# A fused forward and backward kernel: the loads of its start in another order, the transposes of grad_out between their products, and ten blocks of those products ahead of the spectral part

## The chip, the cores and the metric

The kernel runs on one core of a Trainium2 chip. The metric is device time in microseconds (us) of one execution. A core has five engines that work from queues of their own: PE (matmul), DVE (vector), ACT (scalar), POOL (general) and SP, which here only sends transfers. PE's results land in PSUM banks, and ACT or DVE must empty a bank before PE can fill it again. Each engine takes its instructions strictly in the order that the built program gives it.

## The reference: what is computed

The forward part, with S = 2048 tokens, D = 1024 features and F = 3584 hidden units:

```python
mod = (_silu(c) @ w_mod).reshape(c.shape[0], 6, 1, -1)
sa, ca, ga, sb, cb, gb = (mod[:, 0], mod[:, 1], mod[:, 2], mod[:, 3], mod[:, 4], mod[:, 5])
h = _layernorm(x, axis=-1) * (1 + ca) + sa
x = x + ga * _A_ref(h, A_w_r, A_w_i)      # rfft2, times (w_r + i w_i), irfft2
h = _layernorm(x, axis=-1) * (1 + cb) + sb
x = x + gb * _B_ref(h, B_w1, B_b1, B_w2, B_b2)   # layernorm, w1, gelu, w2
```

The outputs are x and the gradients of all inputs for a given `grad_out`. The first step of the backward part needs nothing of the forward part: the gradient that reaches the hidden units, d_ph = (gb * grad_out) w2ᵀ, can be computed as soon as the row gb of `mod` is there. All of this change lies around that product.

## The kernel before, in words

**Rows of mod.** Each of the six rows (0 sa, 1 ca, 2 ga, 3 sb, 4 cb, 5 gb) is computed in two halves. `mod_load` brings 1 MB of weights into one of three tiles in a ring (`wblk`), and `mod_block` (L247) does 8 matmuls (`pm`, L253) with it. Rows 1 and 5 are computed first, row 0 behind the transposes, rows 2, 3 and 4 later.

**gBoT.** `grad_out` comes in four quarters of 512 tokens, `gos[0..3]` (`load_go`). PE transposes each 128x128 piece into a PSUM bank (`pt`, L344, 32 transposes for each quarter, 4 to a bank), and on the way out DVE (L347) and ACT (L351) in turn multiply with the column gb (`gb_col`, made of the row by eight small matmuls `pc`, L337). The result is `gBoT[j]`, j = 0..3.

**pp.** `ph_part(fc, js)` (L673) computes block fc of 28 of d_ph: for each j, eight matmuls (`pp`, L679) of w2ᵀ with `gBoT[j]`, 896 in all, evacuated to `pho` and sent to DRAM (`d_ph`) by POOL. w2ᵀ comes by transposing loads on SP, two blocks to a load, two tiles in turn (`wt`, `load_w2t`, L301). `PH_EARLY` = 6 blocks stand in the program ahead of the spectral part. The other blocks are filler: the scheduler puts their matmuls where PE has nothing else in the spectral part. Of the last four blocks, the j = 2, 3 halves stand in the plan of the next stage.

**x.** Four chunks of 512 rows are loaded (`load_tok`), on SP and on POOL, and go through LayerNorm. `ln_dve` (L437 to L439) takes the statistics on DVE alone, eight for a chunk; `ln_mix` (L447 to L455) takes four on DVE and the others as sums on ACT. `ln_fin` (L427) does the square root on ACT, `norm_act` (L461) the four norms of a chunk on ACT. Then DVE multiplies with the row and folds tokens and features (`fold_tok`, `fold_d`) into `fbuf`. Chunk 0 uses `ln_dve`, the others `ln_mix`.

**Spectral part.** `spectral_core` does the transforms as matmuls: `pu` (L471, 128 matmuls on `fbuf`), `pcs`, a product with the filter on DVE (`R`), `pv`, `po`. Its results are taken by `consume_fwd` (L721), four times: residual, `ln_mix`, `norm_act` from `xt` to `ct`, two products with rows, `ln_dve` on `ct`, `norm_act` from `ct` to `ct`, and a store to `d_n3` on SP.

**The z stage.** `z_block(b, g, g + 1)` (L783) computes 32 matmuls (`pz`, L797) of w1 with the transposed n3 (`n3Ta`, `n3Tb`), four banks, evacuated by ACT (L800), and then the gelu and its derivative: three long ACT operations for a block (L802, L806, L808) between DVE products (L173) and sums (L817). z(b, g) below is such a block. `bo_pass` (L830) does the `pbo` matmuls with w2. The plan (L882) is written out by hand:

```python
plan = [("z", 0, 0)] + [("p", fc, 0) for fc in range(PH_KEEP, NFC)] + [("z", 0, 1), ("z", 0, 2), ("z", 0, 3)]
```

and goes on with `pbo` and further z blocks in turn. So the join of the parts is z(0,0), 64 `pp`, z(0,1), z(0,2), z(0,3), then `pbo` and z(0,4), `pbo` and z(0,5). The loads of w1 are ordered behind the last w2ᵀ load (L751). The rest of the kernel is the backward part.

**What sets the order.** The program is written in one order, and a scheduler gives each engine its own: within `tc.high_priority()` work goes ahead, `tc.issue_after(x)` puts an instruction behind x, and `nc.any` lets the scheduler choose ACT or DVE. So an edit of the start can change the order of ACT and DVE far behind it.

Of the kernel before, what the change touches and what calls it, by code (L numbers as in the profile page):

```python
# [17 lines left out]
P = 128  # L18
# [17 lines left out]
def kernel(  # L36
# [200 lines left out]
    wring = [0]  # L237

# [8 lines left out]
    def mod_block(r, h, wblk=None):  # L247
# [4 lines left out]
        for jc in range(NDC):  # L252
            nc.tensor.matmul(pm[:], lhsT=u_b[:, jc, :], rhs=wblk[:, jc, :], start=(jc == 0), stop=(jc == NDC - 1))  # L253
# [86 lines left out]
    for j in range(4):  # L340
        for cch in range(NDC):
            pt = psum.tile([P, BW], BF16, tag="f", name="pt", bufs=4)
            for a in range(4):
                nc.tensor.transpose(pt[:, a * P:(a + 1) * P], gos[j][:, a, cch * P:(cch + 1) * P], ident[:])  # L344
            if cch % 2 == 0:
                with tc.high_priority():
                    nc.vector.tensor_scalar(out=gBoT[j][:, cch, :], in0=pt[:], scalar1=gb_col[:, cch:cch + 1], scalar2=0.0,  # L347
                                            op0=ALU.mult, op1=ALU.add, accum_out=gu[:, j, cch:cch + 1])
            else:
                with tc.high_priority():  # L350
                    nc.scalar.activation(out=gBoT[j][:, cch, :], in_=pt[:], func=ACT.Identity, scale=gb_col[:, cch:cch + 1],  # L351
                                         accum_out=gu[:, j, cch:cch + 1])

# [297 lines left out]
    for h in range(2):  # L651
        mod_block(0, h)
# [9 lines left out]
    nc.vector.tensor_scalar(out=sar[:, 0], in0=sar[:, 0], scalar1=4.0, scalar2=None, op0=ALU.mult)  # L662
    fold_d(saf.rearrange("p (c d) -> p c d", c=1), sar[:, 0], sar[:, 1])


    pho = reg.tile([P, 3, 4, BW], BF16, name="pho", tag="ot")
    phs = [pho[:, k] for k in range(3)] + [reg.tile([P, 4, BW], BF16, name="phr", tag="ph")[:]]
    last_pe = [None]

    def ordered():  # L670
        return tc.issue_after(last_pe[0].ins)

    def ph_part(fc, js):  # L673
        fg, k = fc // 2, fc % 2
        ph2 = phs[fc % 4]
        for j in js:
            pp = ps_f("pp")
            for cch in range(NDC):
                last_pe[0] = nc.tensor.matmul(pp[:], lhsT=wt[:, fg % 2, cch, k * P:(k + 1) * P], rhs=gBoT[j][:, cch, :],  # L679
                                              start=(cch == 0), stop=(cch == NDC - 1))  # L680
            q = (0, 2, 3, 1)[j]
            ov = ph2[:, :, q * P:(q + 1) * P]
            pv = pp[:, :].rearrange("p (i w) -> p i w", w=P)
            if j % 2 == 0:
                with tc.high_priority():
                    nc.any.tensor_copy(out=ov, in_=pv)
            else:
                with tc.high_priority():
                    nc.any.tensor_copy(out=ov, in_=bass.AP(tensor=pv.tensor, offset=pv.offset + 511, ap=[pv.ap[0], [-P, 4], [-1, P]]))
        if js[-1] == 3:  # L690
            nc.gpsimd.dma_start(out=d_ph[fc * P:(fc + 1) * P, :], in_=ph2.rearrange("p i w -> p (i w)"))

    PH_EARLY = 6
    late_mods = [(r, h) for r in (2, 3, 4) for h in range(2)]
    for fc in range(PH_EARLY):
        ph_part(fc, (0, 1, 2, 3))
        if fc % 2 == 1:
            load_w2t(fc // 2 + 2)
            if fc > 1:
                with tc.issue_after(last_pe[0].ins):  # L700
# [640 lines left out]
```

## Time and profile before

| | |
|---|---|
| median of the runs | 1483.12 us (1481.81 to 1483.87) |
| profiled execution | 1487.43 us, span 1485.5 us |
| PE busy | 1402.2 us, 94% |
| DVE busy | 1069.0 us, 72% |
| ACT busy | 720.3 us, 48% |
| POOL busy | 362.6 us, 24% |
| granted clock of PE, mean | 0.98 |
| read from and written to DRAM | 162.06 MB and 111.20 MB |

Times in the text are counted from the start of the span. A row of a time line gives start, length, engine, line of the kernel, operation, result and operands, the count of instructions put together in the row, and in square brackets the idle time ahead of it and what ended it. A group's name gives tiles without their numbers: `pz` is the bank of a z block. Lines of the kernel before are used for its rows.

Landmarks of before, from the time line of PE: the transposes end at 45.49, the unbroken run of `pu` begins at 128.56, z(0,0) at 346.84, z(0,4) at 392.17, z(0,5) at 406.77.

### The profile page before, as it was taken

Reading aid. Unit: us, or ns where it says so; the run is one execution under the profiler, and the core shown is the slowest. Engines: PE = TensorE matmul, PEld = TensorE weight load, DVE = VectorE, ACT = ScalarE, POOL = GpSimd, SP = SyncE. Lnnn points to the kernel's source line nnn. Section 1 sums busy time; section 2 is a strip of 40 time slices with the busy share of each in tenths; the row PEclk is TensorE's granted clock in tenths of the full one; section 3 lists DMA queues with packets and bytes.
Section 4 is the critical chain, followed back from the end, with each engine's and each line's share of the span. In section 5 each row is a group of like instructions: output and inputs, shape, how many; then the busy total and the mean of one; then the engine's idle time right before and its main releaser. Section 6 shows DMA issues by size and latency. Waiting matters only on the chain.

```text
span 1485.5 us, 18204 instructions
## 1 busy us (share of the span) xinstructions
PE 1402.2 (94%) x6703; PEld 653.7 (44%) x6835; DVE 1069.0 (72%) x1574; ACT 720.3 (48%) x960; POOL 362.6 (24%) x421
## 2 busy tenths in 40 slices
PE   5889989999899999999999999997999999899998
PEld 2434545444344444444344444443444444444443
DVE  5883786898799788887420899986367677888533
ACT  4765546857886756666202333332522444453211
POOL 5620541211113122212111001112134421322323
PEclk8999999999999999999999999999999999999999
DMA  9982563899776876797898266477499977565994
GB/s 335 274 226 61 150 224 122 267 245 338 252 237 213 260 241 219 236 275 230 237 290 253 97 218 227 145 209 196 127 210 246 261 229 213 161 198 154 267 222 169
DMA packets 358046, 324.27 MB, mean 218 GB/s; under 512 B 209066, under 2 KB 300736, under 8 KB 357702
## 3 DMA queue, kind: packets, MB, share of 16 engines
q1 hardware_dynamic: 324166, 207.71, 51.9%
q0 software_dynamic: 33792, 115.40, 22.5%
q8 instruction: 53, 0.87, 0.2%
q14 instruction: 35, 0.29, 0.1%
HBM read 162.06 MB, written 111.20 MB: 184 GB/s over the span
## 4 chain that ended last, share of the span: by engine, by line
PE 32%; DVE 31%; issue 16%; DMA 9%; ACT 8%; POOL 4%; SPq 0%; POOLq 0%; DVEq 0%; ACTq 0%
PE pbo L846 9%; PE pz L797 5%; DVE ct L173 5%; DVE gt L173 4%; PE pu L471 4%; PE pg L943 3%; PE gw2acc L1064 3%; PE pv L564 3%; DVE got L1027 2%; DMA out_dram<-otl 2%; PE gw1acc L1240 1%; ACT ct L461 1%; PE pp L679 1%; DVE st L437 1%; DVE w2sA L817 1%
## 5 line engine op out<-in xcount | busy, mean ns | idle before, releaser
L679 PE MATMUL pp<-gBoT,wt 128*128 128x512 bf16 x878 | 197.4, 381 | 6.4 <-DMA wt<-in_B_w_dram 2.8
L1240 PE MATMUL gw1acc<-gzh,n3n 128*128 128x512 bf16 x876 | 195.2, 381 | 1.2 <-issue 0.2
L943 PE MATMUL pg<-w1T,gzr 128*128 128x512 bf16 x876 | 194.6, 379 | 1.6 <-ACT gn3b L951 0.2
L797 PEld LDWEIGHTS <-w 128*128 128x128 bf16 x896 | 87.6, 98 | 112.5 <-issue 9.0
L679 PEld LDWEIGHTS <-wt 128*128 128x128 bf16 x896 | 88.0, 99 | 110.8 <-issue 6.0
L1240 PEld LDWEIGHTS <-n3n 128*128 128x128 bf16 x896 | 87.7, 98 | 105.7 <-issue 2.5
L943 PEld LDWEIGHTS <-gzr 128*128 128x128 bf16 x896 | 86.8, 98 | 107.9 <-issue 4.9
L797 PE MATMUL pz<-n3Ta,w 128*128 128x512 bf16 x437 | 99.5, 383 | 6.1 <-ACT gt L800 4.1
L1064 PE MATMUL gw2acc<-gB,hhsA 128*128 128x512 bf16 x438 | 99.5, 384 | 3.4 <-DMA hhsA<-d_hh 2.1
L797 PE MATMUL pz<-n3Tb,w 128*128 128x512 bf16 x439 | 98.4, 379 | 0.5
L846 PEld LDWEIGHTS <-hhA 128*128 128x128 bf16 x608 | 59.6, 99 | 74.5 <-issue 5.8
L806 ACT ACTIVATE gt<-gt 128x2048 bf16<-128x2048 bf16 x28 | 53.5, 1910 | 70.9 <-DVE gt L173 70.9
L800 ACT ACTIVATE gt<-pz,b_col 128x512 bf16<-128x512 f32 x112 | 72.8, 684 | 29.1 <-PE pz L797 27.1
L1244 ACT CAST gwo<-gw1acc 128x512 bf16<-128x512 f32 x53 | 30.8, 584 | 115.4 <-PE gw1acc L1240 96.6
L173 DVE TENSOR_TENSOR gt<-gt,gt 128x2048 bf16<-128x2048 bf16 x56 | 68.5, 1223 | 21.6 <-ACT gt L808 20.9
L1069 ACT CAST gwo<-gw2acc 128x512 bf16<-128x512 f32 x54 | 29.9, 583 | 110.9 <-DMA out_dram<-gwo 75.6
L173 DVE TENSOR_TENSOR ct<-ct 128x2048 bf16<-128x2048 bf16 x64 | 75.8, 1219 | 10.7 <-ACT ct L632 8.8
L1064 PEld LDWEIGHTS <-hhsA 128*128 128x128 bf16 x448 | 44.0, 99 | 56.4 <-DMA hhsA<-d_hh 3.8
L987 DVE CUSTOM_DVE_ANT_0 otl<-otl 128x1024 bf16<-128x1024 bf16 x24 | 29.0, 1223 | 51.7 <-DMA otl<-in_w_mod_dram 45.3
L802 ACT ACTIVATE gt<-gt 128x2048 bf16<-128x2048 bf16 x28 | 53.4, 1907 | 0.6
L808 ACT ACTIVATE gt<-gt 128x2048 bf16<-128x2048 bf16 x28 | 53.4, 1907 | 0.5
L1245 POOL DMA_DIRECT2D out_dram<-gwo x56 | 30.7, 550 | 79.6 <-ACT gwo L1244 59.3
(313 smaller groups left out, 2508.5 us busy)
## 6 DMA issues: line engine op xcount, KB each, us to landing
gzr<-d_gz SPq DMA_DIRECT2D x28, 512.0 KB
wblk<-in_w_mod_dram SPq DMA_DIRECT2D x12, 1024.0 KB
out_dram<-otl POOLq DMA_DIRECT2D x48, 256.0 KB
d_ph<-pho POOLq DMA_DIRECT2D x21, 512.0 KB
d_hh<-hhA POOLq DMA_DIRECT2D x19, 512.0 KB
w2sD<-in_B_w_dram SPq DMA_DIRECT2D x14, 512.0 KB
hhC<-d_ph SPq DMA_DIRECT2D x14, 512.0 KB
w2sA<-d_ph SPq DMA_DIRECT2D x14, 512.0 KB
```

The costliest lines, as they stand in the source:

```text
L173: return nc.vector.tensor_tensor(out=out, in0=a, in1=b, op=op)
L471: last_pu[0] = nc.tensor.matmul(pu[:], lhsT=fb[:, i, cl, c8 * P:(c8 + 1) * P], rhs=sm[:, i, :], start=(i == 0), stop=(i == 3))
L679: last_pe[0] = nc.tensor.matmul(pp[:], lhsT=wt[:, fg % 2, cch, k * P:(k + 1) * P], rhs=gBoT[j][:, cch, :], start=(cch == 0), stop=(cch == ...
L797: last_pe[0] = nc.tensor.matmul(pz[:], lhsT=w1s[g][:, cch, k * P:(k + 1) * P], rhs=n3T[:, cch, :], start=(cch == 0), stop=(cch == NDC - 1))
L800: nc.scalar.activation(out=zb[:, k, :], in_=pz[:], func=ACT.Identity, bias=b1_col[:, fc:fc + 1], scale=1.0)
L802: nc.scalar.activation(out=av, in_=zb, func=ACT.Square)
L806: nc.scalar.activation(out=sg, in_=bv, func=ACT.Sigmoid, scale=2.0 * GK)
L808: nc.scalar.activation(out=bv, in_=bv, func=ACT.Sigmoid, scale=-2.0 * GK)
L846: last_pe[0] = nc.tensor.matmul(pbs[i][:], lhsT=hh[:, k, i * P:(i + 1) * P], rhs=wp[:, k, :], start=False, stop=(g == 6 and k == 3))
L943: last_pg[0] = nc.tensor.matmul(pgs[i][:], lhsT=gzs[b, g][:, k, i * P:(i + 1) * P], rhs=w1Ts[g][:, k, h * KH:(h + 1) * KH], start=(g == 0 ...
L1064: nc.tensor.matmul(acc[:], lhsT=hh_of(fc)[:, t, :], rhs=gBs[t // 4][:, t % 4, h * KH:(h + 1) * KH], start=(t == 0), stop=(t == NT - 1))
L1240: nc.tensor.matmul(acc[:], lhsT=n3ns[t // 4][:, t % 4, cch * P:(cch + 1) * P], rhs=gz2[t // 8][:, t % 8, :], start=(t == 0), stop=(t == NT ...
```

## The change

- **Loads on SP.** Before: c, w(1,0), x0, w(1,1), w(5,0), go0, w(5,1), wt0, go1, x1, go2, go3, x2, x3, wt1, then rows 0, 2, 3, 4. After: c, w(5,0), w(5,1), go0, wt0, go1, go2, go3, x0, wt1, w(1,0), w(1,1), x1, x2, w(0,0), x3, wt2, w(0,1), w(2,0) and so on. (w(r,h) is half h of row r of the weights, wt0 the first w2ᵀ load.)
- **PE at the start.** Row 5 first, then the transposes of go0 and go1, the `pp` of j = 0 for blocks 0 and 1 (16 matmuls), the transposes of go2, `pp` of j = 1, the transposes of go3, `pp` of j = 2 and of j = 3. These are tied to that order by `issue_after`.
- **Ten blocks.** `PH_EARLY` is 10. Blocks 2 to 9 follow, with rows (1), (0), (2, and half of 3), (the rest of 3, and 4) of mod between them. In the built order of PE, 264 `pp` stood ahead of the last 120 of the 128 `pu`; now 320 stand ahead of all 128.
- **LayerNorm of x.** The chunk i = 0 stands behind the last DVE evacuation of gBoT, the chunks 1 to 3 behind PE instructions of blocks 1 to 3; which functions they use is as before.
- **What follows from it in the built order.** PE does the same matmuls. ACT has one more table load (8 for 7). At the join, ACT's queue before had the square root and the four last norms of chunk 3 one by one between evacuations of z(0,2) and z(0,3). After, the order of ACT is: two norms of x (`ct<-xt`), the four evacuations of z(0,2), the other two norms of x, two gelu steps, table load and square root, all four last norms (`ct<-ct`), table load, two gelu steps, and then the evacuations of z(0,3).

Cut to its core:

```diff
-    mod_get(1, 0)
-    load_tok(x4s[0], A_x, 0)
-    mod_get(1, 1)
     mod_get(5, 0)
-    for h in range(2):
-        mod_block(1, h, wm[1, h][:])
     mod_get(5, 1)
     load_go(0)
     load_w2t(0)
-    load_go(1)
-    load_tok(x4s[1], A_x, 1)
-    load_go(2)
-    load_go(3)
+    for j in range(1, 4):
+        load_go(j)
     for h in range(2):
         mod_block(5, h, wm[5, h][:])
+    load_tok(x4s[0], A_x, 0)
+    load_w2t(1)
+    mod_get(1, 0)
+    mod_get(1, 1)
+    load_tok(x4s[1], A_x, 1)
     load_tok(x4s[2], A_x, 2)
+    mod_get(0, 0)
+    mod_get(0, 1)
     load_tok(x4s[3], A_x, 3)
-    load_w2t(1)
...
+    def ordered():
+        return tc.issue_after(last_pe[0].ins)
+
+    def ph_part(fc, js):
...
+                with ordered() if fc < 2 else ExitStack():
+                    last_pe[0] = nc.tensor.matmul(pp[:], lhsT=wt[:, fg % 2, cch, k * P:(k + 1) * P], rhs=gBoT[j][:, cch, :],
+                                                  start=(cch == 0), stop=(cch == NDC - 1))
...
+    def go_turned(j):
         for cch in range(NDC):
             pt = psum.tile([P, BW], BF16, tag="f", name="pt", bufs=4)
             for a in range(4):
-                nc.tensor.transpose(pt[:, a * P:(a + 1) * P], gos[j][:, a, cch * P:(cch + 1) * P], ident[:])
+                with ordered() if last_pe[0] is not None else ExitStack():
+                    last_pe[0] = nc.tensor.transpose(pt[:, a * P:(a + 1) * P], gos[j][:, a, cch * P:(cch + 1) * P], ident[:])
...
+    go_turned(0)
+    for j in range(4):
+        if j < 3:
+            go_turned(j + 1)
+        for fc in range(2):
+            ph_part(fc, (j,))
...
-    PH_EARLY = 6
-    late_mods = [(r, h) for r in (2, 3, 4) for h in range(2)]
+    PH_EARLY = 10
+    early_mods = [None, [(1, 0), (1, 1)], None, [(0, 0), (0, 1)], None, [(2, 0), (2, 1), (3, 0)], None, [(3, 1), (4, 0), (4, 1)], None, None]
+    ln_at = {0: gbo_in[0]}
     for fc in range(PH_EARLY):
-        ph_part(fc, (0, 1, 2, 3))
+        if fc > 1:
+            ph_part(fc, (0, 1, 2, 3))
         if fc % 2 == 1:
             load_w2t(fc // 2 + 2)
...
+        for r, h in early_mods[fc] or ():
+            with ordered():
+                mod_block(r, h, wm[r, h][:] if r < 2 else None)
+        if fc in (1, 2, 3):
+            ln_at[fc] = last_pe[0]
...
     for i in range(4):
         x4, fb = x4s[i], fbuf[:, i]
-        if i == 0:
-            with tc.issue_after(u_in.ins):
-                ln_dve(x4, 0, i)
-        elif i > 0:
-            ln_mix(x4, 0, i, fb)
-        else:
-            ln_act(x4, 0, i, fb)
+        with tc.issue_after(ln_at[i].ins):
+            (ln_mix(x4, 0, i, fb) if i > 0 else ln_dve(x4, 0, i))
         norm_act(fb, x4, 0, i)
```

More of the change, by code (lines that the diff above doesn't have):

```diff
@@ L237 @@
     wring = [0]
+    last_pe = [None]
     def mod_tile():
@@ L661 @@
     to_cols(b1_col[:], b1r, NFC, ident[:])
[L662 to L686, printed above, removed]
-            else:
[L688 to L691, printed above, removed]
```

37 lines of the change are left out of this document (26 added, 11 removed).

## The prediction

> **What bounds the kernel now.** I read the page's busy shares first, then the time line of PE, then those of ACT and DVE at the places where PE stands still. The shares:
>
> ```profile
> PE 1402.2 (94%) x6703; PEld 653.7 (44%) x6835; DVE 1069.0 (72%) x1574; ACT 720.3 (48%) x960; POOL 362.6 (24%) x421
> ```
>
> PE leaves only 83 us of 1485.5. Busy time by stretches up to the spectral part (start and end, length, then busy us of PE, PEld, DVE, ACT, POOL; then granted clock, DMA share, GB/s) shows where a third of that lies:
>
> ```profile
> 0.00:20.00 20.00, 7.39 (x22) 2.69 (x23) 10.11 (x28) 3.23 (x5) 16.60 (x35) 0.93 0.92 326
> 20.00:40.00 20.00, 12.35 (x108) 8.48 (x108) 12.33 (x34) 16.04 (x29) 7.12 (x10) 0.82 1.03 350
> ...
> 120.00:128.50 8.50, 7.85 (x36) 3.45 (x36) 7.70 (x8) 2.93 (x5) 0.87 (x2) 1.00 0.28 90
> ```
>
> All stretches to 128.5 sum to 100.4 us of PE: 28 us idle. In the first 40 us the DMA share is 0.92 to 1.03, so this start waits for loads. But the spectral part begins when LN and fold of x are done, on DVE. The time line of DVE there (start, length, operation, count):
>
> ```profile
> 65.21 5.36 DVE L452 TENSOR_SCALAR mv<-mv 128x2 f32<-128x2 f32 x2
> 68.81 1.76 DVE L173 TENSOR_TENSOR fbuf<-x 128x2048 bf16<-128x2048 bf16 x1
> ...
> 126.72 0.69 DVE L173 TENSOR_TENSOR fbuf<-fbuf,sb_saf 128x1024 bf16<-128x1024 bf16 x1
> ```
>
> And of POOL at the first of these rows:
>
> ```profile
> 61.57 8.98 POOL L412 TENSOR_SCALAR em<-em 128x2048 bf16<-128x2048 bf16 x1
> ```
>
> The last piece of fbuf ends at 127.41, and the unbroken run of pu starts at 128.56. The time line of PE, from there to the first blocks of z:
>
> ```profile
> 128.56 12.25 PE L471 MATMUL pu<-smA,fbuf 128*128 128x512 bf16 x55
> ```
>
> ```profile
> 346.84 7.07 PE L797 MATMUL pz<-n3Ta,w 128*128 128x512 bf16 x31
> 353.75 13.98 PE L679 MATMUL pp<-gBoT,wt 128*128 128x512 bf16 x63
> 367.56 20.88 PE L797 MATMUL pz<-n3Ta,w 128*128 128x512 bf16 x94
> ...
> 392.17 7.07 PE L797 MATMUL pz<-n3Ta,w 128*128 128x512 bf16 x31
> ```
>
> ```profile
> 406.77 8.46 PE L797 MATMUL pz<-n3Ta,w 128*128 128x512 bf16 x31 [4.09 <-ACT gt L800]
> ...
> 418.52 7.07 PE L797 MATMUL pz<-n3Ta,w 128*128 128x512 bf16 x31
> ```
>
> At this join ACT serves two masters: it empties the banks of z (L800) and does the last norms of n3 (L461, chunk 3). ACT's time line:
>
> ```profile
> 365.24 1.25 ACT L461 ACTIVATE ct<-xt,stats 128x1024 bf16<-128x1024 bf16 x1
> ...
> 385.53 1.23 ACT L461 ACTIVATE ct<-ct,stats 128x1024 bf16<-128x1024 bf16 x1
> 387.47 1.27 ACT L800 ACTIVATE gt<-pz,b_col 128x512 bf16<-128x512 f32 x2 [0.71 <-DVE hhB L173]
> 388.63 1.24 ACT L461 ACTIVATE ct<-ct,stats 128x1024 bf16<-128x1024 bf16 x1
> ```
>
> Evacuations and norms alternate here, so PE got through z(0,3) and z(0,4) without a stand, and lost 4.09 us only at z(0,5). From 450 to 500 PE is busy for 49.74 of 50: whatever shift z(0,6) (418.52) has is carried to the end.
>
> **The change, part by part.** *Loads.* x0, w(1,0), w(1,1) ahead of the gb weights are gone from the front of SP's queue, x1 goes behind wt1. Landings before: go0 21.5, wt0 26.1, go1 30.1, go2 36.2, go3 39.6, x0 7.6, x3 42.1. A load is 1 MB here, 3.1 us at 340 GB/s (326 and 350 in the rows). Two loads fewer stand ahead of go0, three ahead of wt0, four ahead of go3, and two more ahead of x3; as estimates go0 15, wt0 17, go3 27, x0 30, x3 48, which DVE asks for last. Total bytes are the same, and POOL's own loads stay where they are. wt1 moves up to about 30 (it landed at 47.4); the fourth pp block asks for it after 43.
>
> *Transposes and pp.* The transposes ended at 45.49. Now they alternate with 64 pp (two blocks x 4 j x 8). Estimated end of all of it: 43 (go0 at 15, then 128 transposes at 0.08 us and 64 pp at 0.2135, and the turns of 32 gBoT at 0.67 on DVE and 0.77 on ACT between). The last gBoT is ready at about 41.5 instead of 46.
>
> *Ten blocks ahead.* Before, 264 pp stand ahead of the unbroken pu (192 of six blocks, 72 put in by the scheduler); after, 320. 8 pu that stood among them go behind. So 48 matmuls fewer follow: 48 x 0.2135 = 10.25 us. Ahead of pu, after 43, stand 256 pp and 80 pm: 336 x 0.2135 = 71.7, so PE could start pu at 115. The 56 pp cost nothing because PE idles there; without that cover they would cost 12.0. The 16 us between 115 and pu's start also cover the weights of the other mod rows, which come through the same ring of three tiles, and the stores of d_ph, which POOL sends a little earlier and nobody needs before z.
>
> *LN behind the gBoT.* This is what speaks against it. Before, DVE did 15 of the 20 statistics of x ahead of 46, in the waits for loads; now all 20 of DVE's share (8 + 4 + 4 + 4) stand behind the last gBoT. DVE's work from 45.5 to 128.5 was 10.55 + 19.40 + 17.40 + 16.61 + 7.70 = 71.7, of which 5.3 was the stand in the row at 65.21: 66.4 of its own. Added: 15 statistics at 0.61 (9.2), aggregates (1.2), 8 more evacuations of pp at 0.61 (4.9), less index work (-0.8): 80.9. From 41.5 that ends at 122.4 without one wait. DVE also idled 10.2 us there before. With the same 5.3 stand and 2 of those 10.2 (a fuller queue has less to wait for): 129.7. Plus 1.15 to pu: 131 against 128.56. Bounds: 123.6 (no stand, no wait) and 139 (both in full). I take 131, nearer the middle, since both causes are still there.
>
> The stand: POOL's em operation ran from 61.57 to 70.55, and DVE, after 3.6 us of two-input operations beside it, got nothing done until its end. The Trainium skill (SBUF — State Buffer, "SBUF: two separate sides") says that a GpSimd operation and a DVE operation with two SBUF inputs exclude each other for a whole instruction; the end at 70.55 agrees, the 3.6 us beside each other do not. By that rule statistics and PSUM evacuations, which are not among the operations it names, would pass, and the stand could shrink to nothing if em falls among them; pu would start at 125.7 and the end would be 1485.
>
> *From pu to z.* The filler among pu, pcs, pv and po is the same list, so the interval of 218.28 (128.56 to 346.84) shrinks by 10.25: z(0,0) at 131 + 208.0 = 339.0, 7.8 earlier. The w1 loads hang on the last w2T load, which moves with PE; they stay as far ahead, and PE's 2.80 wait for wt at 333 may grow by up to its own size: I take 1 us.
>
> *The join.* ACT's order is new. Two of the four norms of x for chunk 3 (L461 at 365.24 was the last before) now stand behind the evacuations of z(0,2), and the square root and all four last norms ahead of those of z(0,3), where before they alternated. With z(0,0) at 339.0: z(0,2) ends at 339.0 + 20.7 + 13.9 = 373.6, evacuated 374.4, two norms to 376.7 (before: 366.5). From there DVE does two products with rows, 8 statistics and four gelu products: before 366.52 to 380.2, so 13.7, to 390.3. Square root and the two small DVE operations behind two hhC sums: 392.4. Four norms at 1.13: 397.0. Table load 1.28, L806 and L802 (1.9 each): 402.1. First evacuation 0.6: z(0,4) at 402.8 instead of 392.17, and PE stands from 384.4, 18 us. In return z(0,5)'s 4.09 goes, because DVE and ACT have caught up. z(0,4) then costs 8.3 (the 406.77 row shows a block after a stand), pbo 3.45, z(0,5) 6.9, pbo 3.45: z(0,6) at 424.9 against 418.52 (3.45 is the step from 415.07 to 418.52). Behind the square root in ACT's queue wait those norms, the gelu steps of three blocks and the banks; PE waits for the banks, DVE for the gelu steps.
>
> **Sum.** +6.4, +1 for the weights: +7.4 us. On the profiled execution's 1487.43 that is 1495. The profiled execution lies 4.3 above the median of the runs, 1483.12, and on that median it is 1491 (1490.5). The end moves with pu's start one for one, so it breaks even for a pu at 123.6.
>
> **Rivals.** (a) *Faster: the 10.25 us stay.* PE reaches z(0,4) at 384.4 and ACT has emptied z(0,3) by then. That needs the norms of x done by 358, which needs them ahead of z(0,2): ACT's order forbids it, unless the statistics come far earlier. Price: 10.25 - 2.4 = 8 us, 1475. A milder form is LN at its no-wait bound with the last gBoT at 39 and no wait for weights: pu at 121, the end at -3.6, 1479.5. This form decides for a pu ahead of 120.6. (b) *No difference*: pu at 120.6 to 126.6, the stand gone, 1480 to 1486. (c) *Larger loss*: DVE keeps all its 10.2 of waits and the stand, pu at 139: 8 more than the sum, +15.4, and with the full 2.8 for the weights +17, 1500. For it speaks that norms, gBoT and matrices share ACT up to 60; against it, a fuller DVE queue.
>
> **How the numbers follow.** About 0.2% (3 us) is what a measurement of this kernel can tell from none. Chances: the forecast (1486 to 1495) 0.45, (c) 0.22, (b) 0.13, (a) 0.20. Slower 0.67, same 0.13, faster 0.20. The likeliest one's own range is 1486 to 1495; eight in ten need most of (c) and half of (a): 1475 to 1501.
>
> **What would show it.** 320 pp done ahead of pu; pu's start near 131; z(0,0) near 339; an ACT row with four L496 norms in one group ahead of z(0,3)'s evacuations, and a wait of 14 to 20 us in front of z(0,4), released by ACT. I am wrong if pu starts ahead of 120.6, or if z(0,4) follows pbo without a stand.

## The result, and the profile after

The changed kernel takes 1504.8 us (median of five, 1500.02 to 1505.45) against 1483.12 us before (five, 1481.81 to 1484.93): a ratio of 1.0141, 95% interval 1.0125 to 1.0157, or 21.7 us more. The forecast was 1491.0 us, slower by 7.5 to 8, with a range up to 1501: the sign was right, the loss nearly three times as large, and the time lies 3.8 us above the range. The profiled execution took 1500.02 us (span 1498.2), the fastest of the five, so I read the loss from landmarks inside the trace: z(1,0) starts at 447.62 instead of 428.88 (+18.7), and the first matmul of the later stage `gw2acc` at 992.66 instead of 973.25 (+19.4). What these landmarks show of the loss is nearly all there by z(1,0). The spans of the two profiled executions differ by only 12.7 us, because the part behind `gw2acc` took 505.5 us in this execution and 512.3 in the one of before; over the twenty profiles of this case that part takes between 505.5 and 516.3 us.

Rows of after carry the lines of the changed kernel: `pt` L371, `pp` L352, `pu` L506, `pv` L599, `pz` L803, the evacuation of z L806, the norms L496, the n3 store L741. The shares of busy time on its page:

```profile
PE 1399.3 (93%) x6703; PEld 653.3 (44%) x6835; DVE 1073.7 (72%) x1581; ACT 718.2 (48%) x954; POOL 360.1 (24%) x421
```

The same 6703 matmuls take as long as before; the time went into PE's waits.

**The start.** Two of the stretches that were shown of before (busy time of PE, PEld, DVE, ACT, POOL, then granted clock, DMA share, GB/s):

```profile
0.00:20.00 20.00, 10.66 (x57) 5.77 (x57) 5.13 (x17) 4.98 (x11) 16.01 (x35) 0.88 0.96 243
20.00:40.00 20.00, 10.47 (x84) 7.50 (x87) 9.04 (x24) 10.58 (x22) 3.94 (x5) 0.70 1.08 290
```

DVE and ACT do 14.17 and 15.56 us of work here instead of 22.44 and 19.27: the start became emptier, not fuller. The time line of SP's queue (start, length, operation) says why:

```profile
2.28 1.48 SPq L310 DMA_DIRECT2D go<-in_grad_out_dram  x1
3.80 10.76 SPq L302 DMA_TRANSPOSE wt<-in_B_w_dram  x1
14.61 0.57 SPq L310 DMA_DIRECT2D go<-in_grad_out_dram  x1
```

SP stood 10.76 us in the issue of the transposing load of wt0, with go1 queued behind it. PE's time line shows what waited for go1:

```profile
15.49 1.25 PE L371 MATMUL pt<-ident,go 128*128 128x128 bf16 x10 [2.79 <-DMA go<-in_grad_out_dram]
...
28.72 3.54 PE L371 MATMUL pt<-ident,go 128*128 128x128 bf16 x32 [8.86 <-DMA go<-in_grad_out_dram]
```

go0 came as forecast; go1 was there at 28.72, later than the forecast had go3 (27). The last gBoT was ready at 46.6, no earlier than before. POOL's em operation and DVE beside it, and DVE's last piece of fbuf, each from its engine's time line:

```profile
74.26 5.62 POOL L447 TENSOR_SCALAR em<-em 128x2048 bf16<-128x2048 bf16 x1
```

```profile
73.42 5.80 DVE L173 TENSOR_TENSOR fbuf<-x 128x2048 bf16<-128x2048 bf16 x2
...
130.72 2.36 DVE L173 TENSOR_TENSOR fbuf<-x 128x2048 bf16<-128x2048 bf16 x2
133.12 0.69 DVE L173 TENSOR_TENSOR fbuf<-fbuf,sb_saf 128x1024 bf16<-128x1024 bf16 x1
```

The same pair of operations takes 2.36 us alone and 5.80 us beside em: DVE lost 3.4 us there. From 47 to 133.8 it hardly idled otherwise (1.8 us in its list of waits).

**From pu to the join.** PE's time line, as for before:

```profile
133.87 13.35 PE L506 MATMUL pu<-smA,fbuf 128*128 128x512 bf16 x60 [0.23 <-DVE fbuf L173]
...
343.38 8.41 PE L803 MATMUL pz<-n3Ta,w 128*128 128x512 bf16 x31 [2.79 <-DMA w<-in_B_w_dram]
351.62 13.98 PE L352 MATMUL pp<-gBoT,wt 128*128 128x512 bf16 x63
365.44 13.98 PE L803 MATMUL pz<-n3Ta,w 128*128 128x512 bf16 x63
383.67 8.73 PE L803 MATMUL pz<-n3Ta,w 128*128 128x512 bf16 x31 [4.25 <-ACT gt L806]
...
413.58 9.13 PE L803 MATMUL pz<-n3Ta,w 128*128 128x512 bf16 x31 [17.30 <-ACT gt L806]
...
426.00 7.07 PE L803 MATMUL pz<-n3Ta,w 128*128 128x512 bf16 x31
...
437.26 7.07 PE L803 MATMUL pz<-n3Ta,w 128*128 128x512 bf16 x31 [0.73 <-ACT gt L806]
```

pu starts 5.3 us later than before, z(0,0) 3.5 us earlier, z(0,4) 21.4 us later. PE's waits from 128 to 450 us, before:

```profile
PE pz L797 <- ACT gt L800: 4.1, 1, 4.1
PE pv L564 <- DVE R L173: 3.9, 1, 3.9
PE pp L679 <- DMA wt<-in_B_w_dram: 2.8, 1, 2.8
```

and after (total, times, longest):

```profile
PE pz L803 <- ACT gt L806: 22.3, 3, 17.3
PE pv L599 <- DVE R L173: 5.7, 1, 5.7
PE pz L803 <- DMA w<-in_B_w_dram: 2.8, 1, 2.8
```

With their smaller rows these lists come to 13.7 and 34.2 us: 20.5 more. The three blocks behind a wait also run slower, 8.41, 8.73 and 9.13 us instead of 7.07, 5.1 us together; before one such block, 1.4. That closes the account at z(1,0): pu 5.3 later, less 10.25 of filler that was done earlier, 20.5 more waits and 3.7 of slower matmuls make 19.3, measured 18.7. So PE got 10.25 us less to do in this stretch and waited 20.5 us longer.

What PE waited for stands in ACT's time line at the join:

```profile
380.69 2.35 ACT L496 ACTIVATE ct<-xt,stats 128x1024 bf16<-128x1024 bf16 x2
...
385.23 2.37 ACT L496 ACTIVATE ct<-xt,stats 128x1024 bf16<-128x1024 bf16 x2
...
400.64 0.30 ACT L462 ACTIVATE mv<-mv,eps_c 128x4 f32<-128x4 f32 x1 [8.14 <-DVE mv L473]
403.30 4.63 ACT L496 ACTIVATE ct<-ct,stats 128x1024 bf16<-128x1024 bf16 x4 [2.36 <-DVE stats L173]
...
412.86 2.40 ACT L806 ACTIVATE gt<-pz,b_col 128x512 bf16<-128x512 f32 x4
```

The bank that z(0,4) needs is emptied from 412.86, behind chunk 3's last square root and four norms, in the order that the built program has. But the norms of x, which open this, ended at 387.6, while the forecast had 376.7. DVE's waits from 150 to 420 us show that the chain of the chunks itself was late. The longest rows of both lists are alike: waits for `pcs` and `pv` (29.1 and 11.9 us before, 30.1 and 11.9 after) and of the gelu products for ACT (7.7 before, 8.3 after). The differences stand below them. Before:

```profile
...
DVE Pt L173 <- DMA d_P<-Pt: 2.5, 1, 2.5
DVE ct L173 <- ACT ct L461: 2.5, 3, 1.3
...
DVE ct L173 <- DMA d_n<-ct: 1.4, 2, 0.9
```

After:

```profile
...
DVE ct L173 <- ACT ct L496: 6.6, 2, 5.6
DVE mv L490 <- ACT ct L489: 6.0, 1, 6.0
DVE ct L173 <- DMA d_n<-ct: 5.9, 1, 5.9
DVE Pt L173 <- DMA d_P<-Pt: 4.5, 1, 4.5
```

From pcs to the last square root of chunk 3, a chain of DVE and ACT work in which PE has only the small part of pcs, pv and po, went from 224.7 us (154.47 to 379.2) to 239.8 (160.88 to 400.64).

### The profile page after: what moved, and what is told of

It is laid out like the page before. It is cut to its first block, busy times and chain, and to the rows that moved or that the text cites. A ratio compares the mean times of both kernels' runs of the same rounds, so it can differ in the third digit from the quotient of the medians.

```text
span 1498.2 us, 18196 instructions
## 1 busy us (share of the span) xinstructions
PE 1399.3 (93%) x6703; PEld 653.3 (44%) x6835; DVE 1073.7 (72%) x1581; ACT 718.2 (48%) x954; POOL 360.1 (24%) x421
## 4 chain that ended last, share of the span: by engine, by line
DVE 31%; PE 28%; issue 19%; DMA 8%; ACT 8%; POOL 5%; SPq 0%; POOLq 0%; DVEq 0%; ACTq 0%
PE pbo L852 9%; PE pz L803 5%; DVE ct L173 4%; PE pu L506 4%; DVE gt L173 3%; PE pg L949 3%; PE gw2acc L1070 3%; DVE fbuf L173 2%; DVE got L1033 2%; ACT ct L496 2%; DVE st L472 1%; DMA out_dram<-otl 1%; PE gw1acc L1246 1%; DMA xt<-d_gx 1%; DVE hhC L823 1%
## 5 line engine op out<-in xcount | busy, mean ns | idle before, releaser
L352 PE MATMUL pp<-gBoT,wt 128*128 128x512 bf16 x876 | 195.4, 379 | 4.1 <-DVE pho L362 1.4
L803 PEld LDWEIGHTS <-w 128*128 128x128 bf16 x896 | 88.5, 99 | 137.9 <-issue 34.0
L352 PEld LDWEIGHTS <-wt 128*128 128x128 bf16 x896 | 87.7, 98 | 107.1 <-issue 3.1
L803 PE MATMUL pz<-n3Ta,w 128*128 128x512 bf16 x437 | 104.4, 395 | 27.7 <-ACT gt L806 22.3
L803 PE MATMUL pz<-n3Tb,w 128*128 128x512 bf16 x440 | 98.6, 379 | 0.4
L806 ACT ACTIVATE gt<-pz,b_col 128x512 bf16<-128x512 f32 x112 | 72.3, 684 | 27.0 <-PE pz L803 26.3
```

The lines of the kernel that those rows point to most:

```text
L803: last_pe[0] = nc.tensor.matmul(pz[:], lhsT=w1s[g][:, cch, k * P:(k + 1) * P], rhs=n3T[:, cch, :], start=(cch == 0), stop=(cch == NDC - 1))
L806: nc.scalar.activation(out=zb[:, k, :], in_=pz[:], func=ACT.Identity, bias=b1_col[:, fc:fc + 1], scale=1.0)
```

## The experiments

They ran in groups, each with the kernel before on the same chip; medians and ratios are against those runs. "Chain" is the interval just given; "ahead" counts evacuations and gelu steps of z that ACT does ahead of chunk 3's last norm of x. These and the landmarks are read from the time lines of one profiled execution of each kernel, while the time is the median of its runs.

| kernel | us | ratio, interval | pu starts | z(0,0) | z(0,4) | chain | ahead |
|---|---|---|---|---|---|---|---|
| before | 1483.12 | 1 | 128.6 | 346.8 | 392.2 | 224.7 | 5 |
| after | 1504.8 | 1.0141 (1.0125–1.0157) | 133.9 | 343.4 | 413.6 | 239.8 | 14 |
| e1 | 1507.8 | 1.016 (1.0127–1.0193) | 137.3 | 349.7 | 418.7 | 240.8 | 14 |
| e7 | 1502.6 | 1.0113 (1.0081–1.0144) | 128.0 | 340.5 | 410.6 | 242.0 | 14 |
| e9 | 1489.4 | 1.0031 (1.0017–1.0045) | 136.9 | 354.0 | 401.3 | 226.4 | 5 |
| e10 | 1485.3 | 1.0001 (0.9986–1.0015) | 127.5 | 345.2 | 392.5 | 226.3 | 5 |
| e15 | 1494.9 | 1.005 (1.0031–1.0069) | 128.0 | 346.8 | 394.4 | 230.7 | 8 |
| e13 | 1496.0 | 1.0061 (1.0044–1.0078) | 128.4 | 346.8 | 403.5 | 239.4 | 12 |
| e14 | 1494.8 | 1.005 (1.0033–1.0067) | 127.7 | 346.0 | 399.3 | 235.8 | 10 |
| e16 | 1504.1 | 1.0122 (1.0101–1.0143) | 128.9 | 343.0 | 409.9 | 240.4 | 14 |
| e17 | 1495.4 | 1.0062 (1.0042–1.0083) | 128.0 | 341.1 | 398.8 | 234.3 | 13 |
| e18 | 1493.0 | 1.0048 (1.0022–1.0073) | 128.6 | 350.8 | 405.2 | 238.6 | 8 |

### Which part of the change costs it: e1, e2

Ten early blocks alone, in the kernel before:

```diff
-    PH_EARLY = 6
+    PH_EARLY = 10
```

> The kernel before, with ten blocks ahead of the spectral part instead of six and nothing else; ACT's order at the join becomes that of the changed kernel. Theory J (the loss is made at the join, where ACT's order holds z(0,3)'s banks behind the last norms of chunk 3): the start of before has only 7 us of idle PE between 45.5 and 128.5 for 12.0 us of pp and 1.7 us of pu, so pu ends 5 to 7 us later than before, z(0,4) has a wait of 14 to 20 us released by ACT, and the end is 12 to 22 us above before (1495 to 1505). Theory S (the loss comes from the new order of loads and LayerNorm at the start): within 5 us of before, 1483 to 1488, no wait over 5 us ahead of z(0,4).

1507.8 us, ratio 1.016 (1.0127 to 1.0193). The loads and the transposes are those of before, and z(0,4) has the same wait: 17.49 us, released by ACT. The ten blocks alone bring the whole loss. In the other direction, the changed kernel with six:

```diff
-    PH_EARLY = 10
+    PH_EARLY = 6
```

> The changed kernel with six blocks ahead instead of ten: loads, transposes and LayerNorm as changed, 313 pp end up ahead of the last pu by the scheduler, and ACT's order at the join has two of the four last norms of chunk 3 behind z(0,3)'s evacuations. Theory J: pu starts at about 133 as in the changed kernel, the waits ahead of z(0,3), z(0,4), z(0,5) together fall from 22 to about 10 us, the end falls by 5 to 12 us, to 1493 to 1500. Theory S: the start is the same, so the end is the same, 1503 to 1506.

1502.5 us, ratio 1.0112 (1.0075 to 1.0148): not the 1493 to 1500 that I expected. The scheduler filled the start with `pp` all the same (313 ahead of the last 120 `pu`), and the filler was as thin as with ten. So the number in the source is not what counts; what the two kernels share is how little filler is left behind pu.

### The start: e3, e7

wt0's load behind go3, so that no `go` waits behind a transposing load:

```diff
-    load_go(0)
-    load_w2t(0)
-    for j in range(1, 4):
+    for j in range(4):
         load_go(j)
+    load_w2t(0)
```

> The changed kernel with the first load of w2T behind all four of grad_out instead of behind the first. The wait of 8.9 us for go1 goes, the last gBoT comes at 40 to 42 instead of 46.6. Theory J: DVE's LayerNorm chain, and with it pu, moves up by as much, pu at 127 to 129; ACT's order at the join is the same, so the whole chain to z(0,4) moves up one for one and the end falls by 4 to 6 us, to 1498 to 1501. If the end is set by something else at the join than the chain that starts with pu: no change, 1503 to 1506, with the wait ahead of z(0,4) longer by 4 to 6.

1500.5 us, ratio 1.0116 (1.0086 to 1.0146). go1's transposes start at 19.61 instead of 28.72, pu at 130.33, z(0,4) at 411.54: 2.0 us of the 21.4. pu moved up by 3.5 us (to 127 to 129 was expected), and z(0,4) did not follow one for one. With that, LayerNorm of x tied as before (chunk 0 behind the first work of DVE, the others free):

> The changed kernel with the first load of w2T behind grad_out and with LayerNorm of x tied as before (chunk 0 behind the first DVE work, the others free), so that DVE can take statistics in its waits for loads. From pu on, all orders are those of the changed kernel. Theory J: pu comes 2 to 6 us ahead of the run with the moved load alone (130.3), at 124 to 128, z(0,4) still at pu + 281, the end 2 to 6 us below that run's 1500.5, 1494 to 1499. If the statistics are not what delays fbuf: pu at 130, 1500.

1502.6 us, ratio 1.0113 (1.0081 to 1.0144): a miss, I expected 1494 to 1499. The start is wholly repaired: pu at 127.98 and z(0,0) at 340.47, both earlier than in the kernel before. z(0,4) still starts at 410.56, 18.4 us later than before. The interval from pu to z(0,4) is 282.6 us here, 279.7 in after, and 263.6 before. The loss is made behind pu.

### ACT's order at the join, the forecast's cause: e4, e6, e8, e5, e11

In e4 ACT has no part in chunk 3's last LayerNorm: DVE does the square root by three Newton steps and the norms as `tensor_scalar`, in a new function `ln_norm_dve`:

```diff
...
-        ln_dve(tmp, 2, i)
-        norm_act(tmp, tmp, 2, i)
+        if i == 3:
+            ln_norm_dve(tmp, 2, i)
+        else:
+            ln_dve(tmp, 2, i)
+            norm_act(tmp, tmp, 2, i)
```

> The changed kernel with the last LayerNorm of chunk 3 taken off ACT: the square root by three Newton steps on DVE and the four norms on DVE, some 3 to 4 us more for DVE, and two table loads, one square root and four norms (7.5 us and the waits for DVE) less for ACT. Theory J: ACT empties z(0,3) without those 20 us between; the wait ahead of z(0,4) falls from 17 to 3 to 10 us and the end by 7 to 14, to 1491 to 1498. Theory S: no change, 1503 to 1507.

1501.6 us, ratio 1.0126 (1.0095 to 1.0157), where 1491 to 1498 were expected. z(0,4) came at 407.23, and ACT now waited 12.87 us for DVE at 400.95: the stand had moved to the other queue. In e6 both LayerNorms of chunk 3 go ahead in the scheduler's order:

```diff
+        with tc.high_priority() if i == 3 else ExitStack():
             ln_mix(x4, 1, i, tmp)
             norm_act(tmp, x4, 1, i)
...
             norm_act(tmp, tmp, 2, i)
```

> The changed kernel with the two LayerNorms of chunk 3 at high priority: in ACT's queue the four norms of x alternate with the evacuations of z(0,2), the last norms of chunk 2 go behind them, and z(0,3) is emptied between the two pairs of the last norms. Two more table loads (2.6 us). Theory J: the norms of x end 3 to 6 us earlier and two norms fewer (2.3 us) stand ahead of z(0,3)'s banks; z(0,4) at pu + 272 to 277, the end 3 to 8 us lower, 1496 to 1501. If the order at the join does not matter: 1502 to 1507.

1502.6 us, ratio 1.0115 (1.0076 to 1.0155), another miss (1496 to 1501). z(0,4) starts at 405.77, but 4.06 us are lost again at z(0,5), and z(1,0) starts at 446.6, 1.0 us ahead of after. The same edit in the kernel before:

> The kernel before with the same high priority for chunk 3's LayerNorms, six blocks ahead and the old start: all four norms of x and the last norms of chunk 2 go ahead of z(0,1), the last norms of chunk 3 alternate with the evacuations of z(0,1) and z(0,2), none stands near z(0,3). Theory J: the wait of 4.1 us ahead of z(0,5) goes or moves, 0 to 5 us faster than before, 1478 to 1484. If ACT's order there is not on the path: no change.

1485.6 us, ratio 0.9998 (0.9983 to 1.0012): nothing. So at this start and this filler, the order of the last norms is not what decides. Two further suspects: the n3 stores on POOL's queue instead of SP's (e5), and all 64 `pp` of the plan ahead of z(0,0) (e11):

```diff
-        nc.sync.dma_start(out=chunk_rows(d_n3, i), in_=tmp)
+        nc.gpsimd.dma_start(out=chunk_rows(d_n3, i), in_=tmp)
```

> The changed kernel with the four stores of n3 sent by POOL instead of SP, so that the second one no longer stands in SP's ring behind the last two loads of w2T. Theory J, refined by the first runs (from pu to z(0,4) the chain that ends in chunk 3 takes 281 us whatever the start, against 265 before; 5.9 us of that is DVE waiting for the second store of n3 to land): the wait falls below 2 us, z(0,4) comes at pu + 275 to 278, the end falls by 3 to 6 us, to 1498 to 1501. If ACT's order alone sets z(0,4): no change, 1502 to 1505, and a longer wait of DVE for ACT behind it.

1500.5 us, ratio 1.01 (1.007 to 1.013), in the range expected but not in the way expected: DVE still waited 4.6 us for the store instead of 5.9 (below 2 was expected), so its place in SP's queue is not the main part.

```diff
-    plan = [("z", 0, 0)] + [("p", fc, 0) for fc in range(PH_KEEP, NFC)] + [("z", 0, 1), ("z", 0, 2), ("z", 0, 3)]
+    plan = [("p", fc, 0) for fc in range(PH_KEEP, NFC)] + [("z", 0, g) for g in range(4)]
```

> The changed kernel with the 64 pp of the plan ahead of z(0,0) instead of behind it, so that z(0,0) to z(0,3) stand together and z(0,0)'s gelu work comes 14 us later. PE's work is the same. Theory C: chunk 3 goes further ahead in the queues of ACT and DVE, the four norms of x come ahead of z(0,2) and z(0,3) is emptied between the two pairs of the last norms; z(0,4) 3 to 8 us earlier than 413.6, the end 1497 to 1502. Theory P: the same 1502 to 1506.

1498.8 us, ratio 1.0103 (1.0074 to 1.0132), as expected. z(0,0) starts at 357.12, but the blocks behind it then wait 10.04 and 6.91 us for ACT.

### Giving the filler its work back: e9, e10, e12, e15

If the filler's size decides, useless work in it must gain time. In the filler, blocks 17 to 23 compute their j = 0 product twice; the second pass overwrites the first, the result is the same, and PE has 56 matmuls more, 12.0 us at 0.2135:

```diff
             pp = ps_f("pp")
+            if j == 0 and 17 <= fc < 24:
+                for cch in range(NDC):
+                    last_pe[0] = nc.tensor.matmul(pp[:], lhsT=wt[:, fg % 2, cch, k * P:(k + 1) * P], rhs=gBoT[j][:, cch, :],
+                                                  start=(cch == 0), stop=(cch == NDC - 1))
```

> The changed kernel with 56 matmuls of no use among the filler (the first quarter of blocks 17 to 23 is computed twice, 12.0 us of PE), so that PE reaches z(0,0) as late behind pu as before. Theory C (from pu on, the chain of DVE and ACT that ends in chunk 3's LayerNorms sets the end, and PE waits for it 24 us at the join; z blocks that start early put their gelu work ahead of chunk 3 in the queues of DVE and ACT): the added 12 us are free or better, z(0,0) at 352 to 356, the waits ahead of z(0,1) to z(0,5) together fall from 22 to 12 us or less, the end between 1492 and 1505, not above the changed kernel. Theory P (PE's own work sets the end and the waits are fixed by ACT's order): 12 us more, 1514 to 1518.

1489.4 us (ten runs), ratio 1.0031 (1.0017 to 1.0045), better than the 1492 to 1505 expected. With 12 us more work on PE the changed kernel is 15 us faster. PE's time line of e9 (`pz` L807, evacuation L810):

```profile
353.99 6.85 PE L807 MATMUL pz<-n3Ta,w 128*128 128x512 bf16 x31
...
401.30 7.07 PE L807 MATMUL pz<-n3Ta,w 128*128 128x512 bf16 x31
...
416.85 9.24 PE L807 MATMUL pz<-n3Ta,w 128*128 128x512 bf16 x31 [5.03 <-ACT gt L810]
```

z(0,0) starts 10.6 us later than in after and z(0,4) 12.3 us earlier, without a wait. ACT's time line (norms L500, square root L466):

```profile
375.90 1.25 ACT L500 ACTIVATE ct<-xt,stats 128x1024 bf16<-128x1024 bf16 x1
...
390.25 0.30 ACT L466 ACTIVATE mv<-mv,eps_c 128x4 f32<-128x4 f32 x1 [1.23 <-DVE mv L477]
...
400.97 2.38 ACT L500 ACTIVATE ct<-ct,stats 128x1024 bf16<-128x1024 bf16 x2
```

Although its pu starts 3.0 us later, chunk 3's last norm of x ends 10.45 us earlier than in after, and the last square root comes 10.39 us earlier: the chain takes 226.4 us again. The same on top of e7, where the start is repaired too:

> The same 56 matmuls of no use in the kernel with ten blocks, the first load of w2T last and LayerNorm of x tied as before (1502.6). There pcs begins at 155.6, 1.2 us behind the kernel before, and with the 56 matmuls PE has before's work between pu and z. Theory C: the chain gets before's cover back, z(0,4) within 8 us of before's 392.2, the end 1484 to 1494, 8 to 18 us faster for 12 us more work. Theory P: 1513 to 1517.

1485.3 us (ten runs), ratio 1.0001 (0.9986 to 1.0015): the time of the kernel before, with 56 matmuls more. The start, which was worth nothing that could be told without the useless work (after to e7), is worth 4.1 us with it (e9 to e10). The same 56 in the kernel before:

> The control: the kernel before with the same 56 matmuls of no use. Before, PE waits only 4.1 us at the join (z(0,5)) and 1 to 4 us at each of a few other places, so under both theories most of the 12.0 us must show: 8 to 12 us slower than before, 1491 to 1498.

1492.1 us, ratio 1.0043 (1.003 to 1.0056). The time is in the range expected, but the 12.0 us cost only 6.8, less than the 8 to 12 expected. So in the kernel before the filler was long enough for most of the added work to cost time, and even there a part of it was cover. Last, 32 instead of 56 on top of e7 (blocks 17, 19, 21, 23):

> e10 with 32 useless matmuls instead of 56 (blocks 17, 19, 21 and 23, j = 0, computed twice: 6.9 us of TensorE instead of 12.0; the result stays the same). If the loss follows TensorE's work evenly, the time lies between e7's 1502.6 and e10's 1485.3 in proportion, at 1491 to 1494 us. If it is a matter of which order the queues get, it is a step: within 3 us of either end.

1494.9 us, ratio 1.005 (1.0031 to 1.0069): about half the loss, close to proportion (1491 to 1494 was expected) and not by a step; the chain is at 230.7 us. z(0,4) is nearly back to its place (394.4), and PE now waits 6.91 us for ACT ahead of z(0,5).

### What in the chain gets longer: e13, e14, e16, e17, e18

Two things in the chain differ visibly. Chunk 3's unfold waits 5.5 us for an n3 store, and more of z's work stands ahead of chunk 3 on ACT. ACT's square roots divide the chain into links; here are their starts, counted from pcs:

| square root of | before | after | e10 | e7 | e7 less e10 |
|---|---|---|---|---|---|
| chunk 1, last LayerNorm | 155.0 | 158.4 | 159.7 | 161.0 | 1.3 |
| chunk 2, LayerNorm of x | 173.0 | 182.0 | 175.9 | 184.2 | 8.3 |
| chunk 2, last LayerNorm | 197.4 | 205.1 | 199.7 | 207.3 | 7.6 |
| chunk 3, LayerNorm of x | 204.9 | 216.4 | 206.1 | 218.6 | 12.5 |
| chunk 3, last LayerNorm | 224.7 | 239.8 | 226.3 | 242.0 | 15.7 |

e7 and e10 differ by the useless work alone. Of the 15.7 us, 8.3 are there at chunk 2's square root for x, at 339.85 in e7, and z(0,0) begins only at 340.47. So z's operations can't be the cause of that half. Most of it is the wait for the store; SP, DVE and ACT in e7:

```profile
312.68 11.78 SPq L302 DMA_TRANSPOSE wt<-in_B_w_dram  x2
324.76 0.51 SPq L743 DMA_DIRECT2D d_n<-ct  x1
```

```profile
336.78 2.36 DVE L173 TENSOR_TENSOR ct<-ct 128x2048 bf16<-128x2048 bf16 x2 [5.46 <-DMA d_n<-ct]
```

```profile
339.85 0.30 ACT L461 ACTIVATE mv<-mv,eps_c 128x4 f32<-128x4 f32 x1 [6.02 <-DVE mv L489]
```

and SP in e10:

```profile
314.36 2.06 SPq L302 DMA_TRANSPOSE wt<-in_B_w_dram  x1
322.55 0.39 SPq L747 DMA_DIRECT2D d_n<-ct  x1
331.62 1.82 SPq L302 DMA_TRANSPOSE wt<-in_B_w_dram  x1
```

With less filler the last `wt` load goes out ahead of the store instead of behind it, since it waits for `pp` to be done with its tile. In e10 the unfold doesn't wait at this store. The other 7.4 us come in behind z's start. That wait is no necessary part of the loss, though: in e2 the waits for two such stores are 1.25 and 0.98 us, and its chain takes 242.0 us all the same.

All five experiments start from e7. e13 holds the first w1 load until DVE has begun that unfold, by a 2-element `memset`:

```diff
...
+        if g == 0:
+            with tc.issue_after(unf[0].ins):
+                nc.vector.memset(wtile[:, 0, 0:2], 0.0)
         with tc.issue_after(w2t_in[0].ins):
             nc.sync.dma_start(out=wtile[:], in_=w1_v[:, :, g * BW:(g + 1) * BW])
```

> The kernel is the changed one with wt's first load last and the LayerNorms tied as before (e7, 1502.6 us), and the first w1 load is held until VectorE has begun chunk 3's unfold, so that w1's stream can't run beside the n3 store that this unfold waits for. Two theories of what lengthens pu to z(0,4) from 264 to 281 us. L, the landing: the unfold's wait of 5.5 us for the n3 store is a term of its own; it falls below 1.5 us, z(0,4) starts at 405 to 407 instead of 410.6, and the time is 1497 to 1499 us. O, the order: an early chunk 3 meets the same gelu work ahead of it in ScalarE's and VectorE's queues, z(0,4) stays within 2 us of 410.6, and the time is 1501 to 1504 us.

1496.0 us, ratio 1.0061 (1.0044 to 1.0078): 6.6 below e7, but not in the way that I meant. The scheduler sent the loads of w1's blocks 1 and 2 ahead of the held one; the unfold still waited 6.3 us. What the hold did was to keep z(0,0) back until 346.75, 6.3 us later than in e7. PE waited 8.65 us for w1, and z(0,4) still started 7.1 us earlier. e14 adds e6's priority:

> As e13, and chunk 3's two LayerNorms go ahead in the planner's order. If landing and order together are the loss, z(0,4) starts at 400 to 403 us and the time is 1490 to 1495 us, without one useless matmul. If TensorE's work in the filler is needed in itself, as cover for the rest of the chain (z's own gelu work and the blocks behind it), the time stays above 1498 us.

1494.8 us, ratio 1.005 (1.0033 to 1.0067), at the upper end of what landing and order together should give, with the landing still at 6.0. e16 puts all other w1 loads behind the held one, which tests the landing alone:

```diff
-        with tc.issue_after(w2t_in[0].ins):
-            nc.sync.dma_start(out=wtile[:], in_=w1_v[:, :, g * BW:(g + 1) * BW])
+        with tc.issue_after(w2t_in[0].ins if g == 0 else w1_in[0].ins):
+            w1_in.append(nc.sync.dma_start(out=wtile[:], in_=w1_v[:, :, g * BW:(g + 1) * BW]))
...
```

> In e13 the planner sent the loads of w1's blocks 1 and 2 ahead of the held one, beside the n3 store, so the unfold still waited 6.3 us. Here all w1 loads stand behind the held one. L, the landing: the wait falls below 2 us, chunk 3's last square root moves from 395.5 to about 391 us, z(0,4) from 403.5 to 398 to 400, and the time from 1496.0 to 1490 to 1493 us. O, the order alone: the wait falls, but z(0,4) stays at 402 to 405 and the time at 1494 to 1498 us.

1504.1 us, ratio 1.0122 (1.0101 to 1.0143), above both forecasts, and the wait was still 5.0 us: w1 is not the main part of what makes the store late. z(0,0) is at 342.99, 3.8 us ahead of e13's, and the loss is whole again. e17 adds the priority:

> e16 with chunk 3's two LayerNorms first in the planner's order (e14 with all w1 loads held). Landing and order as terms that add: z(0,4) at 393 to 396 us, 1487 to 1491 us. If the landing's price is covered by the later waits on ScalarE: within 2 us of e14's 1494.8.

1495.4 us, ratio 1.0062 (1.0042 to 1.0083), within 2 us of e14 and 8.7 below e16: with a repaired start, the order of chunk 3's norms is worth what it was not in e6. In e17 two transposing loads of wt stood ahead of the store on SP's queue; e18 puts the last one behind it:

```diff
-            load_w2t(fc // 2)
+            with tc.issue_after(n3_st[1].ins) if fc == NFC - 2 else ExitStack():
+                load_w2t(fc // 2)
...
```

> e17, and the last transposing load of wt is queued on SyncE behind chunk 1's n3 store; in e17 two of these loads stood ahead of the store, and the unfold of chunk 3 still waited 4.1 us. If these loads are what makes the store land late, the wait falls below 1.5 us; the filler's last products then wait some 3 us for wt, which the idle at z(0,4) covers, and the time falls from 1495.4 to 1490 to 1493 us. If a later wait on ScalarE covers the landing, the wait falls and the time stays within 2 us of 1495.4.

1493.0 us, ratio 1.0048 (1.0022 to 1.0073), which can't be told from e17. DVE's waits from 300 to 350 us, e17:

```profile
DVE ct L173 <- DMA d_n<-ct: 4.1, 1, 4.1
```

and e18:

```profile
DVE stats L465 <- ACT mv L463: 7.1, 1, 7.1
...
DVE ct L173 <- DMA d_n<-ct: 0.6, 1, 0.6
```

So the transposing load ahead of it is what made the store late. But the edit brought a wait of its own, which ACT's time line of e18 shows:

```profile
342.98 0.59 ACT L360 CAST pho<-pp 128x512 bf16<-128x512 f32 x1 [8.82 <-PE pp L353]
343.46 0.30 ACT L463 ACTIVATE mv<-mv,eps_c 128x4 f32<-128x4 f32 x1
```

PE waited 8.98 us for the load that was moved, an evacuation of `pp` on ACT waited for PE, and chunk 2's square root stood behind that evacuation in ACT's order; DVE waited 7.1 us for it. PE's time line of e18 (`pz` L815):

```profile
391.78 9.65 PE L815 MATMUL pz<-n3Ta,w 128*128 128x512 bf16 x32 [6.25 <-ACT gt L818]
...
405.15 7.07 PE L815 MATMUL pz<-n3Ta,w 128*128 128x512 bf16 x32
```

The first of these rows is z(0,3); z(0,4) is at 405.15, 6.4 us later than in e17, and the chain takes 238.6 us against 234.3. So what the landing of the store is worth by itself is not shown: e18 put another, longer wait in its place.

**What follows.** Shown: the loss lies between pu and the first blocks of z (e7), it comes with the thin filler (e1), and it goes when the filler gets useless work (e9, e10), about in proportion (e15). Two edits that let z come later or chunk 3 go first on a repaired start take back 7 to 9 of the 17 us between e7 and e10 without a matmul more (e13, e17 against e16). How the chain gets longer is shown in part only. About half of it is there before z begins, with the late store; that this half would go with the store's wait is not shown (e2, e18). For the other half there is a reading of the table. Where few of z's operations stand ahead of chunk 3's last norm of x on ACT (before, e9, e10: 5) the chain takes 225 to 226 us; where 12 to 14 do, it takes 234 to 242. When PE comes to z early, z's evacuations and gelu steps get their places in the queues of ACT and DVE among the work of chunks 2 and 3, which z(0,4)'s banks wait for in the end. The count does not rank the kernels alone (e18: 8 and 238.6). The useless work gives PE something to do and also changes the order that the scheduler builds for ACT and DVE, and no run separates the two. Nor is the chain alone on the path in the kernel before: e8 shortens it to 217.9 us and gains nothing. It stays open what the other 8 to 10 us between e17 or e18 and e10 are made of; no kernel here got all of them back without more work on PE. None was faster than the kernel before.

## Why the prediction was wrong in size

- **The loads.** go0 at 15 was right (first transpose at 15.49). The last gBoT at 41.5 was wrong: 46.6. The working counted bytes and places in SP's queue, but not the 10.76 us that SP stood in the issue of the transposing load with go1 behind it; before, such rows of 12.88 and 12.39 us stood in the same view. With the ties of LayerNorm it is worth 2 to 4 us (e3, e9 to e10).
- **Ten blocks.** 320 `pp` ahead of pu, as said. The 16 us of cover in front of pu were not there: PE finished its last `pp` there at about 132.9, a microsecond ahead of fbuf. It cost nothing yet, but only just.
- **LN behind the gBoT.** Right in its terms: DVE's own work came to about 82 us (85.2 busy from the last gBoT to the end of fbuf, less the stand) against 80.9, the stand to 3.4 against 5.3, pu to 133.87 against 131. The last gBoT came 5.1 us later than forecast, and the smaller stand took a part of that back. The rival by which the stand vanishes did not come about. The Trainium skill (SBUF — State Buffer, "SBUF: two separate sides") has a GpSimd operation and a two-input DVE operation exclude each other for a whole instruction. The 3.4 us that DVE lost beside em agree with that in the main. The prediction held against this rule that DVE did 3.6 us of such work beside em before; but em took 8.98 us there and 5.62 here, 3.36 less, so these rows agree too if em itself was waiting for DVE.
- **From pu to z.** 208.0 us forecast, 209.5 measured, w1's wait of 2.79 included where 1 was taken. Right for PE.
- **The join, the step that failed.** "Two norms to 376.7" was timed from z(0,2)'s end on PE, as if chunk 3 moved with PE's filler. Measured: 387.6, which is 10.9 us later, and z(0,4) at 413.58 instead of 402.8, 10.8 later. Of the 10.9, 5.8 come from PE, which ended z(0,2) at 379.42 instead of 373.6 (pu 2.9 late, 1.5 more from there to z(0,0), 1.4 more from z(0,0) to the end of z(0,2), most of it in the slow first block). The other 5.1 come from the chain: ACT did chunk 3's square root for x at 377.25, and the first two norms of x and the evacuation of z(0,2) stood behind it. Between the norms of x and z(0,4) the working held: 15.7 us from the end of the norms of x to the last norms, forecast and measured. The chain of the chunks runs on DVE and ACT, and it became longer instead of earlier: 239.8 us against 224.7. I read PE's filler as work on the path, which gets shorter by 10.25 us; it was cover for the longer chain beside it. z(0,5)'s wait went, as said. That the wait for z(0,4) has the size forecast, 17.30 us released by ACT against 18, is luck: PE came to it at 396.28 instead of 384.4 and the bank 10.8 us late, so both ends of the wait moved by about as much. The wait of 4.25 us ahead of z(0,3) was not forecast.
- **The cause.** The forecast laid the wait on ACT's order of the last norms alone. Taking that away left the time at 1501.6 and 1502.6 (e4, e6). ACT's queue is where the loss shows; why it is late lies further back.
- **The clock.** The forecast had slower matmuls behind a wait for z(0,4) alone (8.3 us, measured 9.13), not for the blocks at 343.38 and 383.67. In the 6 us from 340 the granted clock was 0.72 and in the 9.2 us from 413.5 it was 0.77, and 31 matmuls took up to 9.13 us instead of 7.07: 3.7 us more than before in all. The Trainium skill (TensorE: Matmul & The Clock Gate, "What's actually happening") puts PE back to half speed after an idle window of about 3.4 us. The waits of 4.25 and 17.30 agree with that. The wait of 2.79 is shorter than this window, and yet the granted clock was 0.50 from 343 to 346 behind it, while behind a wait of 2.80 in the kernel before (`pp` at 333.01) it stayed at 1.00.

## What to carry to other kernels

Work that an engine does while it waits for a longer chain is worth nothing when it is taken away, and moving it can cost more than its size: what stands behind it comes early, here a load that went out ahead of a store of the chain, and operations of the next stage that got in among the chain's in the other engines' queues. Before moving filler, measure the chain beside it from its first to its last link: if the chain and not the filler sets the end, an engine with 94% of the span is still not the bound there. A cheap test is useless work in the filler: if the kernel gets no slower by it, or even faster, the filler was cover. Read the orders of the other engines beside it, since the scheduler may change them with the work that PE is given.

## What the runs showed of the hardware

A transposing load of w2ᵀ held SP's queue for 10.76 us at the start of after, for 14.44 in e3 and for 12.88 and 12.39 before, and the next transfer of SP was issued only then. Plain loads of this start took from 0.4 us (the first of `wblk`) to 5.14 (x0 in after), and transposing loads later in the kernel took less than 2 us in places (1.86 at 288.81 before). A store of 1 MB behind two such loads (e17) kept DVE waiting 4.1 us, while behind one of them (e18) the wait was 0.6, although the other load followed it at once. It is not the place in SP's queue that does it: with the store on POOL's queue (e5) and the two loads on SP's ahead of it in time, the wait was 4.6.
